# A fused convolution and gated feed-forward kernel: the conv bands built in 128x32 tiles, a late conv step, and the first weight slice loaded as fp32

## The chip, the cores and the metric

The kernel runs on one core of one Trainium2 chip. The metric is the device time of one execution in microseconds (us). Five engines matter: TensorE (PE in the profile, PEld for its weight loads), VectorE (DVE), ScalarE (ACT), GpSimd (POOL) and SyncE (SP, which here only issues DMAs). SyncE, ScalarE and GpSimd each issue their DMAs from the same in-order queue that holds their other instructions; for ScalarE the profile calls that queue ACTq.

## The reference

`x` is (8, 4096, 192), all in fp32. First comes a causal convolution over 7 taps with one set of softmax-normalised weights for each of 8 heads (24 channels each), then a gated feed-forward layer with 1536 hidden columns:

```python
w = exp(weight - max(weight)); w = w / (sum(w) + 1e-9)            # (8, 7)
out = einsum('hk,bskhg->bshg', w, windows(x_pad, 7))              # conv
x = out.reshape(B * S, D)
gate = maximum(x @ w_gate, 0); val = x @ w_val
return (gate * val) @ w_out                                       # (32768, 192)
```

## The kernel before

The 32768 tokens are worked in 16 units of 1024 tokens of each of two streams (batches 0 to 3 and 4 to 7). A unit runs `gate_val` for two windows of 512 tokens (matmuls of L621: for each of 12 blocks `f` of 128 hidden columns, gate and val, three chunks `c` of 64 channels, two streams `st`), then the projection (L643). The schedule is manual: each engine runs its instructions in the order in which the code is written, and the framework adds the semaphore waits.

The convolution of most windows is done by ScalarE, VectorE and GpSimd beside the matmuls of earlier units. For the first windows there is no earlier unit, so TensorE does it, with banded matrices. This head of the program is where the change lies. Its steps are:

- `load_raw` (L109) loads the first window's five overlapping pieces of x, called pieces 0 to 4 here, as fp32: 1, 0, 3, 4 by SyncE's queue and 2 by ScalarE's, after the small `w8`. In the tables of order the tiles `prod_86` to `prod_90` are pieces 0 to 4. `cast` (L119) turns each into fp16 on ScalarE, in the order 1, 0, 2, 3, 4.
- A small matmul (L203) spreads the conv weights, VectorE takes the maximum (L275), ScalarE the exponential `e` (L278) and its sum (L281), and VectorE makes `blocks` from them (L287 to L299), three pieces for heads 0-2, 3-5 and 6-7.
- L335: for each of the three `BANDS`, 8 matmuls with shifted selections from `Z` as weights (128x128) add `blocks` into a PSUM bank; VectorE copies each out to `bands` (L343).
- `conv_steps` (L391): 8 small matmuls (tiles of 32 columns) for each chunk `c` and piece; pieces 0, 1, 2, 3, 4 give columns 0, 106, 212, 318, 424 onwards of a 512-column window. Three chunks and five pieces make 120 matmuls.
- `evict` (L402) copies the three chunks from PSUM to `dense[0]`, chunk 0 and 2 on ScalarE and chunk 1 on VectorE.
- `load_w` (L224) loads the weights in four slices (columns 0-127, 128-383, 384-767, 768-1535) by GpSimd's queue, which turns fp32 into fp16, into partitions 0 to 63 of `Wg` and `Wv`. Stream 1 needs a copy in partitions 64 to 127: `both_halves` (L231) makes it, blocks 0 and 1 on VectorE, 2 to 9 on GpSimd (`pool_halves`), 10 and 11 by a DMA.
- `load_x` (L97) loads x for the second conv group (`xts[1]`, window 1 of unit 0) in two DMAs on GpSimd's queue, one for each stream. TensorE convolves it at block 10 of the first window (`CONV1`).

In the first block of the first window the L621 matmuls go by chunk: chunk 0 gate, chunk 0 val, chunk 1 gate, and so on, two matmuls (streams) at each step. So chunk 0's copy and both weight blocks are needed first, and chunk 1's copy two steps later.

Of the kernel before, what the change touches and what calls it, by code (L numbers as in the profile page):

```python
# [8 lines left out]
FP = mybir.dt.float32  # L9
# [6 lines left out]
def kernel(  # L16
# [12 lines left out]
    nc = tc.nc  # L29
# [7 lines left out]
    NCH = D // 64  # L37
    NBLK = D // 32
    NFF = DFF // 128
    WIN = 512  # L40
    NWIN = S // WIN
    SUB = 112
    STEP = 106
# [2 lines left out]
    GSUB = 5  # L46
    WARM = [(4, 4, 4, 1), (4, 4, 1)]
    STEPS0 = [1, 0, 2, 3, 4]
    CONV1 = 10


# [5 lines left out]
    LPOOL = NCH * WIN - LDVE  # L57
# [12 lines left out]
    apool = ctx.enter_context(tc.tile_pool(name="apool", bufs=1))  # L70
# [13 lines left out]
    def load_x(g, streams=range(2)):  # L84


        bp, toks = GROUPS[g]
        xt = staged(g // 3, g % 3).rearrange("p (j s d) -> p j s d", s=2, d=D)
        step = toks[1] - toks[0]
        rows = -(-(step + PAD) // 16) * 16  # L90
        for st in streams:
            src = bass.AP(
                tensor=x.tensor,
                offset=x.offset + ((bp + NB * st) * S + toks[0] - PAD) * D,
                ap=[[D, rows], [step * D, len(toks)], [1, D]],
            )
            nc.gpsimd.dma_start(out=xt[0:rows, 0 : len(toks), st, :], in_=src)  # L97
        return xt

    xts = {0: staged(0, 0).rearrange("p (j s d) -> p j s d", s=2, d=D)}  # L100
# [5 lines left out]
    def load_raw(queue, jj):  # L106
        lo = STEP * jj - PAD
        p0 = max(0, -lo)
        queue.dma_start(  # L109
            out=raw[jj][p0 : ROWS[jj], :].rearrange("p (s d) -> p s d", s=2),  # L110
            in_=bass.AP(
                tensor=x.tensor,
                offset=x.offset + (lo + p0) * D,
                ap=[[D, ROWS[jj] - p0], [NB * S * D, 2], [1, D]],
            ),
        )
# [7 lines left out]
    HR = 128 // H  # L124
# [5 lines left out]
    for jj in (1, 0, 3, 4):  # L130
        load_raw(nc.sync, jj)
    load_raw(nc.scalar, 2)

    zeros = const.tile([128, 128], F16)
    nc.vector.memset(zeros[:], 0.0)
# [21 lines left out]
    Z = const.tile([128, 256], F16)  # L157
# [3 lines left out]
    with nc.allow_low_precision("one of the terms is not zero"):  # L161
        nc.vector.tensor_reduce(
            out=Z[:, 112 : 112 + HR],
            in_=eye[:].rearrange("p (g i) -> p i g", i=HR),
# [4 lines left out]
        out=mask[:, :, 0],  # L169
        in_=eye[:].rearrange("p (g i) -> p g i", i=HR),  # L170
# [4 lines left out]
    Wg = const.tile([128, NCH, DFF], F16)  # L175
    Wv = const.tile([128, NCH, DFF], F16)
    Wo = const.tile([128, NFF, 3, 64], F16)
    nc.vector.memset(Wg[0:1, 0, 0:1], 0.0)

    held = psum.tile([128, 2, 512], FP, name="ps")  # L180

# [26 lines left out]
    for part, heads in zip(raised, BANDS):  # L208
        nc.tensor.matmul(  # L209
            out=part[:, 0 : SUB * len(heads)],  # L210
            lhsT=zeros[:],
            rhs=none(len(heads), SUB),
            start=True,
            stop=False,
# [6 lines left out]
    def load_w(s):  # L221
        cols = slice(CUTS[s], CUTS[s + 1])
        for src, dst in ((moe_w_gate, Wg), (moe_w_val, Wv)):
            nc.gpsimd.dma_start(  # L224
                out=dst[0:64, :, cols],
                in_=src.rearrange("(c p) f -> p c f", p=64)[:, :, cols],
            )

    def both_halves(copy, s, dst):
        cols = slice(HALVES[s], HALVES[s + 1])  # L230
        copy(out=dst[64:128, :, cols], in_=dst[0:64, :, cols])  # L231

    def pool_halves(s):
        both_halves(nc.gpsimd.tensor_copy, s, Wg)
        both_halves(nc.gpsimd.tensor_copy, s, Wv)
# [32 lines left out]
            )  # L268
        xes[b] = xe, head

    for s in range(2):
        load_w(s)

    mx = const.tile([128, 1], FP)
    nc.vector.tensor_reduce(  # L275
        out=mx[:], in_=spread[:, 0, 0:KW], axis=mybir.AxisListType.X, op=ALU.max, negate=True
# [34 lines left out]
    for s in range(2, 4):  # L311
        load_w(s)
    pool_halves(2)
    xts[1] = load_x(1, range(1))
    for s in (3, 4, 5):
        pool_halves(s)
    load_x(1, range(1, 2))
    for s in (6, 7):
        pool_halves(s)
# [8 lines left out]
    for part, heads, to, copy in zip(  # L328
        raised, BANDS, bands, [nc.vector.tensor_copy] * 3
    ):  # L330
        n = len(heads)
        for j in range(128 // HR):
            s0 = HR * j - PAD
            lo, hi = max(0, -s0), min(BW, SUB - s0)
            nc.tensor.matmul(  # L335
                out=part[:, 0 : SUB * n].rearrange("p (h t) -> p h t", t=SUB)[:, :, s0 + lo : s0 + hi],
                lhsT=Z[:, 112 - HR * j : 240 - HR * j],
                rhs=blocks[:, heads[0] : heads[0] + n, lo:hi],
                start=False,
                stop=(j == 128 // HR - 1),  # L340
                skip_group_check=True,
            )
        copy(out=to[:].rearrange("p h t -> p (h t)"), in_=part[:, 0 : SUB * n])  # L343
# [54 lines left out]
                            skip_group_check=True,  # L398
                        )

    def evict(copy, g, ps, c):
        copy(out=dense[0][:, g, c, :], in_=ps[:, 0, :])  # L402

    def conv(g):

# [301 lines left out]

    dense[0] = xcpool.tile([128, 2, NCH, WIN], F16, name="xc")
    first = [psum.tile([128, 2, 512], FP, name="ps") for _ in range(NCH)]
    for c, steps in ((0, STEPS0[:3]), (1, STEPS0[:2]), (0, STEPS0[3:]), (1, STEPS0[2:]), (2, STEPS0)):  # L710
        conv_steps(0, first[c], c, steps)
    both_halves(nc.vector.tensor_copy, 0, Wg)
    both_halves(nc.vector.tensor_copy, 0, Wv)
    for c, copy in enumerate((nc.scalar.copy, nc.vector.tensor_copy, nc.scalar.copy)):
        evict(copy, 0, first[c], c)
    both_halves(nc.vector.tensor_copy, 1, Wg)
    both_halves(nc.vector.tensor_copy, 1, Wv)
    xts[2] = load_x(2)
# [82 lines left out]
```

## Time and profile before

| | |
|---|---|
| median of 3 runs | 761.82 us (761.52 to 762.06) |
| span of the profiled execution (first to last instruction) | 760.2 us |
| the median over that span | 1.62 us more |
| PE busy | 756.0 us (99%), 13724 matmuls |
| DVE busy | 675.8 us (89%) |
| ACT busy | 610.1 us (80%) |
| POOL busy | 461.3 us (61%) |

The profile gives the span of the profiled execution and no time of its own beside it; the 1.62 us between the span and the median of the other runs lies before the first and behind the last instruction, or is the difference of two executions. A row of a timeline reads: start, length, engine, line, operation, output<-input with partitions x elements, how many instructions were merged, and in brackets the idle time of the engine just before it with what ended it. A line with x4 merges four instructions that follow each other.

### The profile page before, as it was taken

To read this page: it belongs to the slowest core of one execution; us is meant where nothing else is said; L and a number is where in the kernel's file an instruction comes from. 1 tells how busy PE (TensorE), PEld (TensorE's weight loads), DVE (VectorE), ACT (ScalarE), POOL (GpSimd) and SP (SyncE) were. 2 spreads that over 40 slices of the span, in tenths; PEclk is the share of its full clock that TensorE was granted. 3 is DMA by queue.
4 is the path that set the end of the run, shared out by engine and by line. 5 is a ranking of instruction groups with operands and counts; after the bars stand their busy time and mean duration, and the time that the engine had idled before them with its cause. 6 is when DMAs were issued, how large, how long until landed. Compare 5 with 4: busy or idle time off the path is not lost.

```text
span 760.2 us, 30531 instructions
## 1 busy us (share of the span) xinstructions
PE 756.0 (99%) x13724; PEld 454.8 (60%) x13724; DVE 675.8 (89%) x647; ACT 610.1 (80%) x680; POOL 461.3 (61%) x311
## 2 busy tenths in 40 slices
PE   9999999999999999999999999999999999999998
PEld 5555555565565666656666565666656556566658
DVE  7889989998998989989999899998999989897891
ACT  7897887878878788887877878788797887877671
POOL 8729649195591946829377392874919659193600
PEclk9999999999999999999999999999999999999999
DMA  8953532345324443333434324352243531240302
GB/s 142 137 69 92 79 85 46 43 96 75 85 44 52 97 66 85 55 61 83 60 85 71 66 67 55 85 85 69 56 49 93 77 86 44 23 100 9 85 2 85
DMA packets 153714, 54.07 MB, mean 71 GB/s; under 512 B 148912, under 2 KB 153584, under 8 KB 153584
## 3 DMA queue, kind: packets, MB, share of 16 engines
q1 hardware_dynamic: 117376, 37.78, 21.6%
q0 software_dynamic: 35808, 14.07, 16.4%
q8 instruction: 107, 1.75, 1.0%
q10 hardware_dynamic: 400, 0.27, 0.1%
q14 instruction: 23, 0.19, 0.1%
HBM read 28.98 MB, written 25.17 MB: 71 GB/s over the span
## 4 chain that ended last, share of the span: by engine, by line
PE 99%; DMA 0%; ACT 0%; issue 0%
PE ps L621 65%; PE ps L643 31%; PE ps L686 2%; PE ps L391 0%; DMA w<-in_weight_dram 0%; PE ps L193 0%; PE ps L335 0%; PE ps L414 0%; PE ps L209 0%; PE ps L203 0%; ACT out_s L697 0%; ACT L127 0%
## 5 line engine op out<-in xcount | busy, mean ns | idle before, releaser
L633 DVE TENSOR_TENSOR hT<-gr,ps 128x1024 f16<-128x1024 f16 (+1 forms) x385 | 469.1, 1219 | 35.5 <-ACT gr L632 8.7
L632 ACT ACTIVATE gr<-ps 128x1024 f16<-128x1024 f32 (+1 forms) x385 | 392.8, 1021 | 114.4 <-PE ps L621 114.4
L550 POOL TENSOR_TENSOR prod<-prod,prod 128x896 f32<-128x896 f32 x145 | 302.6, 2087 | 251.8 <-DVE prod L584 242.7
L621 PE MATMUL ps<-xc,Wg 64*64 64x512 f16 (+1 forms) x4464 | 318.4, 376 | 0.0
L621 PE MATMUL ps<-xc,Wv 64*64 64x512 f16 (+1 forms) x4464 | 318.3, 376 | 0.0
L643 PE MATMUL ps<-hT,Wo 64*64 64x512 f16 x4320 | 235.8, 376 | 0.0
L621 PEld LDWEIGHTS <-Wv 64*64 64x64 f16 (+1 forms) x4464 | 149.9, 106 | 98.5 <-DVE hT L633 0.3
L621 PEld LDWEIGHTS <-Wg 64*64 64x64 f16 (+1 forms) x4464 | 145.4, 107 | 103.4 <-issue 0.2
L643 PEld LDWEIGHTS <-Wo 64*64 64x64 f16 x4320 | 137.3, 107 | 95.7
L538 ACT ACTIVATE prod<-x_r,tap 128x1024 f32<-128x1024 f16 (+2 forms) x195 | 182.7, 1017 | 0.0
L574 DVE SCALAR_TENSOR_TENSOR acc<-x_r,tap,acc 128x1024 f32<-128x1024 f16 (+3 forms) x150 | 118.0, 854 | 0.0
L661 DVE STREAM_TRANSPOSE out_s<-ps 128x1024 f32<-128x1024 f32 x45 | 56.2, 1248 | 28.4 <-PE ps L643 24.4
L550 POOL TENSOR_TENSOR xc<-prod,prod 128x896 f16<-128x896 f32 x29 | 60.6, 2089 | 2.3
L479 POOL COPY x_p<-x_e 128x1536 f16<-128x1536 f16 (+1 forms) x32 | 42.2, 1351 | 0.0
L251 POOL DMA_DIRECT2D x_e<-in_x_dram x30 | 26.6, 890 | 0.0
L574 DVE SCALAR_TENSOR_TENSOR xc<-x_r,tap,acc 128x1024 f16<-128x1024 f16 (+3 forms) x30 | 25.2, 840 | 0.0
L563 ACT ACTIVATE acc<-x_r,tap 128x1024 f32<-128x1024 f16 (+3 forms) x30 | 22.5, 800 | 0.0
L656 ACT COPY turned_by<-ps 128x2 f32<-128x2 f32 x45 | 7.0, 155 | 16.8 <-PE ps L643 14.8
L686 PEld LDWEIGHTS <-hT 128*128 128x128 f16 x192 | 15.8, 98 | 0.4 <-issue 0.4
L686 PE MATMUL ps<-Wo,hT 128*128 128x192 f16 x192 | 16.0, 246 | 0.0
L697 ACT COPY out_s<-ps 128x768 f32<-128x768 f32 (+2 forms) x5 | 3.2, 638 | 12.7 <-PE ps L686 12.7
L697 DVE COPY out_s<-ps 128x192 f32<-128x192 f32 x1 | 0.4, 359 | 13.3 <-PE ps L686 13.3
(61 smaller groups left out, 74.4 us busy)
## 6 DMA issues: line engine op xcount, KB each, us to landing
out_dram<-out_s SPq DMA_DIRECT2D x125, 192.0 KB
x_e<-in_x_dram POOLq DMA_DIRECT2D x28, 384.0 KB, 6.3
x_r<-x_p SPq DMA_TRANSPOSE x116
prod<-in_moe_w_out_dram POOLq DMA_DIRECT2D x1, 576.0 KB, 8.7
prod<-in_x_dram SPq DMA_DIRECT2D x3, 168.0 KB
out_dram<-out_s SPq DMA_DIRECT2D x5, 96.0 KB
out_s<-in_x_dram POOLq DMA_DIRECT2D x2, 210.0 KB, 6.2
out_s<-in_x_dram POOLq DMA_DIRECT2D x2, 192.0 KB, 6.1
```

The source lines that it names most:

```text
L251: nc.gpsimd.dma_start(out=xe[:, 0:n, st, :, :].rearrange("p j c r -> p j (c r)"), in_=bass.AP(tensor=x.tensor, offset=x.offset + row * D, ...
L479: nc.gpsimd.tensor_copy(out=xp[:, js, :, st, :], in_=xe[:, js, st, :, :])
L538: nc.scalar.activation(out=both(prods[b, k], b, at, n), in_=shifted(b, c, k, t, n), func=ACTF.Copy, scale=tap[:, c, k : k + 1],)
L550: nc.gpsimd.tensor_tensor(out=acc if k < KW - 1 else xcs[b][:, w, :, :].rearrange("p c t -> p (c t)")[:, LDVE : NCH * WIN], in0=acc, in1=p ...
L563: nc.scalar.activation(out=both(accs[b], b, at, n), in_=shifted(b, c, 0, t, n), func=ACTF.Copy, scale=tap[:, c, 0:1],)
L574: nc.vector.scalar_tensor_tensor(out=result(b, at, n) if k == KW - 1 else both(acc, b, at, n), in0=shifted(b, c, k, t, n), scalar=tap[:, c ...
L621: nc.tensor.matmul(out=pss[i][q : q + M, st, :], lhsT=W[64 * st : 64 * st + 64, c, 128 * f + q : 128 * f + q + M], rhs=xcb[64 * st : 64 * ...
L632: nc.scalar.activation(out=gr[:, sts], in_=pss[0][:, sts], func=ACTF.Relu)
L633: nc.vector.tensor_tensor(out=h[:, f, sts], in0=gr[:, sts], in1=pss[1][:, sts], op=ALU.mult)
L643: nc.tensor.matmul(out=ps[64 * st : 64 * st + 64, b, :], lhsT=Wo[64 * r : 64 * r + 64, f, p, :], rhs=hs[b][64 * r : 64 * r + 64, f, st, :] ...
L661: nc.vector.transpose(out=o[:].rearrange("p t (b d) -> p b t d", b=2)[:, :, :, 32 * p : 32 * p + 32], in_=ps[:].rearrange("p b (t c) -> p ...
L686: nc.tensor.matmul(out=ps[:, i // 2, D * (i % 2) : D * (i % 2) + D], lhsT=h[:, f, st, 128 * q : 128 * (q + 1)], rhs=Wo[:, f, :, :].rearran ...
```

## The change

Four edits, all in the head:

1. The band matmuls (L335) use 32 columns of weights each, placed by `tile_position` in one quarter of the array, and write 32 partitions of the bank, in the order 0, 2, 4, 6, 1, 3, 5, 7 (`PLACED`), so that four neighbours lie in four quarters.
2. The first weight slice (128 columns) isn't loaded by GpSimd any more. SyncE issues two DMAs for gate and ScalarE two for val, fp32, one into each half of the partitions of a tile `sent` (it takes the buffer of `prod6`), and VectorE casts both halves at once into `Wg` and `Wv`, in place of its two `both_halves` copies. GpSimd's first weight DMA is now that of slice 1.
3. `conv_steps` for chunks 0 and 1 takes pieces 1, 0, 2, 3 first and piece 4 last. Chunks 0 and 1 are copied out in two parts: columns 0 to 317 and 318 to 511, on VectorE and ScalarE for chunk 0, on ScalarE and VectorE for chunk 1.
4. The first of the two `load_x` DMAs for the second group is issued behind blocks 3, 4, 5 of GpSimd's copies rather than ahead of them.

```diff
+    PLACED = [0, 2, 4, 6, 1, 3, 5, 7]
...
     load_raw(nc.scalar, 2)
+    sent = apool.tile([128, 2 * LPOOL], FP, name="prod6")[:, 0 : 2 * NCH * 128].rearrange(
+        "p (i c f) -> p i c f", i=2, c=NCH
+    )
+    for i, (queue, src) in enumerate(((nc.sync, moe_w_gate), (nc.scalar, moe_w_val))):
+        for half in (slice(0, 64), slice(64, 128)):
+            queue.dma_start(
+                out=sent[half, i],
+                in_=src.rearrange("(c p) f -> p c f", p=64)[:, :, 0:128],
+            )
...
-    for s in range(2):
-        load_w(s)
+    load_w(1)
...
     pool_halves(2)
-    xts[1] = load_x(1, range(1))
     for s in (3, 4, 5):
         pool_halves(s)
+    xts[1] = load_x(1, range(1))
     load_x(1, range(1, 2))
...
-        for j in range(128 // HR):
+        for j in PLACED:
+            q = HR * j // 32 * 32
...
-                lhsT=Z[:, 112 - HR * j : 240 - HR * j],
+                lhsT=Z[:, 112 - HR * j + q : 144 - HR * j + q],
                 rhs=blocks[:, heads[0] : heads[0] + n, lo:hi],
                 start=False,
-                stop=(j == 128 // HR - 1),
+                stop=(j % 2 == 1),
+                tile_position=(0, q),
...
-    for c, steps in ((0, STEPS0[:3]), (1, STEPS0[:2]), (0, STEPS0[3:]), (1, STEPS0[2:]), (2, STEPS0)):
+    for c, steps in ((0, STEPS0[:4]), (1, STEPS0[:4]), (0, STEPS0[4:]), (1, STEPS0[4:]), (2, STEPS0)):
         conv_steps(0, first[c], c, steps)
-    both_halves(nc.vector.tensor_copy, 0, Wg)
-    both_halves(nc.vector.tensor_copy, 0, Wv)
-    for c, copy in enumerate((nc.scalar.copy, nc.vector.tensor_copy, nc.scalar.copy)):
-        evict(copy, 0, first[c], c)
+    early_cols, late_cols = slice(0, 3 * STEP), slice(3 * STEP, WIN)
+    evict(nc.vector.tensor_copy, 0, first[0], 0, early_cols)
+    for i, dst in enumerate((Wg, Wv)):
+        nc.vector.tensor_copy(out=dst[:, :, 0:128], in_=sent[:, i])
+    evict(nc.scalar.copy, 0, first[0], 0, late_cols)
+    evict(nc.scalar.copy, 0, first[1], 1, early_cols)
+    evict(nc.vector.tensor_copy, 0, first[1], 1, late_cols)
+    evict(nc.scalar.copy, 0, first[2], 2)
```

What the built programs hold at the two places that matter is shown next; line numbers of the changed kernel are 1 to 13 higher. The names in brackets are the semaphores that an instruction waits for: `DMAHW0` to `DMAHW7` are eight counters that the DMAs of SyncE and ScalarE take in turn, `DMASW` those of GpSimd's DMAs, the others count an engine's finished instructions.

On ScalarE, at the program's start, stood before:

```order
L129 DMA w_93<-in_weight_dram 8x7
L109 DMA prod_88<-in_x_dram 112x2x192
L278 ACTIVATE e<-ps,mx 128x7 [waits DVE_49]
L281 ACTIVATE total,sm<-e 128x8 [waits Activation_49]
L119 CAST out_s<-prod_87 112x384 [waits DMAHW0_49]
L119 CAST out_s<-prod_86 118x384 [waits DMAHW1_49,Pool_49]
```

and stands now (`prod_100` is `sent`):

```order
L130 DMA w_93<-in_weight_dram 8x7
L110 DMA prod_88<-in_x_dram 112x2x192
L139 DMA prod_100<-in_moe_w_val_dram 64x3x128
L139 DMA prod_100<-in_moe_w_val_dram 64x3x128 [waits DMAHW1_49]
L287 ACTIVATE e<-ps,mx 128x7 [waits DVE_49]
L290 ACTIVATE total,sm<-e 128x8 [waits Activation_49]
L120 CAST out_s<-prod_87 112x384 [waits DMAHW0_49]
L120 CAST out_s<-prod_86 118x384 [waits Pool_49]
```

Two DMAs stand ahead of the exponential. There are now ten DMAs of SyncE and ScalarE for eight counters; the tenth is ScalarE's second, it shares the counter `DMAHW1` with the load of piece 0, and waits until that load has landed. The cast of piece 0 (`prod_86`) has lost its own wait for that load, since ScalarE has already waited.

On VectorE, behind the three copies of the bands, stood before:

```order
L343 CAST band_188<-ps 128x336 [waits PE_49]
L343 CAST band_189<-ps 128x336 [waits PE_49]
L343 CAST band_190<-ps 128x224 [waits PE_49]
L231 COPY Wg<-Wg 64x3x128 [waits DMASW0_49]
L231 COPY Wv<-Wv 64x3x128 [waits DMASW1_49]
L402 CAST xc<-ps 128x512 [waits PE_49]
```

and stands now:

```order
L356 CAST band_191<-ps 128x336 [waits PE_49]
L356 CAST band_192<-ps 128x336 [waits PE_49]
L356 CAST band_193<-ps 128x224 [waits PE_49]
L415 CAST xc<-ps 128x318 [waits PE_49]
L728 CAST Wg<-prod_100 128x3x128 [waits DMAHW6_49,DMAHW0_49]
L728 CAST Wv<-prod_100 128x3x128 [waits DMAHW7_49,DMAHW1_49]
L415 CAST xc<-ps 128x194 [waits Activation_49]
```

while ScalarE, behind its five casts, where two whole chunks stood, now holds:

```order
L120 CAST out_s<-prod_90 96x384 [waits DMAHW4_49]
L415 CAST xc<-ps 128x194 [waits DVE_49]
L415 CAST xc<-ps 128x318 [waits PE_49]
L415 CAST xc<-ps 128x512 [waits PE_49]
```

The second part of each chunk waits for the other engine's copy of its first part (`DVE_49` on ScalarE for chunk 0, `Activation_49` on VectorE for chunk 1), so the two parts of a chunk follow each other. The first part of chunk 0 waits for TensorE's count 107 in the built program: 35 up to the bands, 32 for chunk 0's four pieces, 32 for chunk 1's, and 8 for chunk 0's piece 4. So it waits for the whole chunk, piece 4 among it, and not for its own columns alone; the first part of chunk 1 likewise waits for 115.

More of the change, by code (lines that the diff above doesn't have):

```diff
@@ L177 @@
     Wo = const.tile([128, NFF, 3, 64], F16)
-    nc.vector.memset(Wg[0:1, 0, 0:1], 0.0)
+    nc.vector.memset(Wg[0:1, 0, 128:129], 0.0)
     held = psum.tile([128, 2, 512], FP, name="ps")
@@ L335 @@
             nc.tensor.matmul(
-                out=part[:, 0 : SUB * n].rearrange("p (h t) -> p h t", t=SUB)[:, :, s0 + lo : s0 + hi],
-                lhsT=Z[:, 112 - HR * j : 240 - HR * j],
+                out=part[q : q + 32, 0 : SUB * n].rearrange("p (h t) -> p h t", t=SUB)[
+                    :, :, s0 + lo : s0 + hi
+                ],
+                lhsT=Z[:, 112 - HR * j + q : 144 - HR * j + q],
                 rhs=blocks[:, heads[0] : heads[0] + n, lo:hi],
                 start=False,
-                stop=(j == 128 // HR - 1),
+                stop=(j % 2 == 1),
+                tile_position=(0, q),
                 skip_group_check=True,
@@ L399, in conv_steps, with evict @@
                         )
-    def evict(copy, g, ps, c):
-        copy(out=dense[0][:, g, c, :], in_=ps[:, 0, :])
+    def evict(copy, g, ps, c, cols=slice(0, WIN)):
+        copy(out=dense[0][:, g, c, cols], in_=ps[:, 0, cols])
     def conv(g):
```

## The prediction

> **What bounds the kernel now.** I read the chain that ended last first: it says which engine the end hangs on, and where that engine ever waited.
>
> ```profile
> PE 99%; DMA 0%; ACT 0%; issue 0%
> ...
> 7.81 13.22 PE ps L621 x120
> 21.03 1.64 PE ps L391 x120
> 22.66 18.28 PE ps L621 x168
> ...
> 88.61 15.54 PE ps L643 x288
> 104.15 31.09 PE ps L621 x575
> ...
> 710.22 31.08 PE ps L621 x576
> ```
>
> From 7.81 us on TensorE runs through without a wait that the chain shows, and each later unit has the same lengths, 31.08 and 15.54. So no edit of the head can gain or lose anything but by the moment at which the first L621 matmuls run, and whatever delays them goes to the end one for one. The two pieces ahead of the conv group (L391 at 21.03) bound what could be caught up. Next I read the timelines of ScalarE, VectorE and TensorE over the first 9 us, to see which wait ends last ahead of 7.81.
>
> ```profile
> 0.87 0.59 ACTq L129 DMA_DIRECT2D w<-in_weight_dram  x1
> 1.50 0.34 ACTq L109 DMA_DIRECT2D prod<-in_x_dram  x1
> 3.55 0.27 ACT L278 ACTIVATE e<-ps,mx 128x7 f32<-128x7 f32 x1 [1.25 <-DVE mx L275]
> 4.06 1.78 ACT L119 CAST out_s<-prod 112x384 f16<-112x384 f32 x4
> 6.18 0.51 ACT L119 CAST out_s<-prod 96x384 f16<-96x384 f32 x1 [0.34 <-DMA prod<-in_x_dram]
> 7.17 0.58 ACT L402 CAST xc<-ps 128x512 f16<-128x512 f32 x1 [0.48 <-PE ps L391]
> ...
> 5.56 1.22 DVE L343 CAST band<-ps 128x336 f16<-128x336 f32 x3 [0.26 <-PE ps L335]
> 6.81 0.39 DVE L231 COPY Wg<-Wg 64x384 f16<-64x384 f16 x1
> 7.44 0.69 DVE L402 CAST xc<-ps 128x512 f16<-128x512 f32 x1
> ...
> 4.97 1.22 PE L335 MATMUL ps<-blocks,Z 128*128 128x48 f16 x24
> 6.12 1.68 PE L391 MATMUL ps<-band,out_s 112*32 112x106 f16 x120
> 7.81 0.39 PE L621 MATMUL ps<-xc,Wg 64*128 64x512 f16 x2
> 8.24 0.40 PE L621 MATMUL ps<-xc,Wg 64*128 64x512 f16 x2
> ```
>
> The chain through the head: exponential at 3.55, band matmuls at 4.97, band copies from 5.56, conv from 6.12, chunk 0's copy on ScalarE from 7.17 to 7.75, first L621 matmul at 7.81, chunk 1's first at 8.24, 0.11 after VectorE's copy of chunk 1 ends at 8.13. The weights came in time and were copied by VectorE ahead of that. The exponential started when the maximum came, and ScalarE had been idle 1.25 us for it.
>
> **The wait on ScalarE.** The order shows a DMA ahead of the exponential that waits for the load of piece 0. When that load lands is in the view of line L119 over 4.1 to 4.3 us, because the cast of piece 0 had the same wait, and as the only cast with two waits it kept one as a row of its own in ScalarE's queue.
>
> ```profile
> L119 ACTq EVENT_SEMAPHORE  x1: 17/17/17, 4.1 to 4.1; - x1
> ...
> L109 SPq DMA_DIRECT2D prod<-in_x_dram x4: 398/454/458, 0.8 to 2.3; - x4
> L109 ACTq DMA_DIRECT2D prod<-in_x_dram x1: 339/339/339, 1.5 to 1.5; - x1
> ```
>
> The wait ended at 4.1; before, it held nothing, since the first cast ran until about then. Now the DMA behind it takes 0.34 to 0.59 us to issue (the rows of loads from DRAM, 0.59 that of `w`); I take 0.40, near most of them. So the exponential starts at about 4.55, **1.0 us later**. Behind it wait its sum, all five casts, and through VectorE the whole making of the bands.
>
> **The bands and the conv.** All else equal the band matmuls start at 4.97 + 1.0 = 5.97. The 24 took (1.22 - 0.2 for the length of the last) = 1.02 us start to start, 0.043 each, so the 8 of one band 0.34. Now four run side by side; L391's tiles of the same width ran at (1.68 - 0.21)/120 = 0.012 each, so two rounds of four are about 0.1. The first band copy then starts 0.59 - 0.25 = 0.34 behind the matmuls, at 6.31. It can't gain more: the copies follow each other every 0.42 (1.22 for three, the last 0.38), so they start at 6.31, 6.73, 7.15 and end at 6.81, 7.23, 7.53. **Gain of this edit: 0.25 us.**
>
> Conv starts 0.06 behind the first copy, at 6.87. Chunk 0's four pieces (32 matmuls at 0.0125) end at 7.27, chunk 1's start at 7.29 with the second band and end at 7.69, chunk 0's piece 4 at 7.79. The casts don't hold it: five of them, 0.42 apart, from 4.06 + 1.0 on, the last ends at 7.26. Nor does the load of piece 4, which landed at 6.18 before (two weight DMAs now compete with it).
>
> **The copies out.** Their lengths come from copies of near sizes:
>
> ```profile
> L343 DVE CAST band<-ps 128x336 f16<-128x336 f32 x2 | 0.9, 502 | 0.3 <-PE ps L335 0.3
> ...
> 755.30 0.48 ACT L697 COPY out_s<-ps 128x384 f32<-128x384 f32 x1 [1.18 <-PE ps L686]
> 756.29 0.36 DVE L697 COPY out_s<-ps 128x192 f32<-128x192 f32 x1 [13.32 <-PE ps L686]
> 757.28 0.32 ACT L697 COPY out_s<-ps 128x192 f32<-128x192 f32 x1 [1.50 <-PE ps L686]
> ```
>
> As the order stands, the parts form one string, all behind piece 4: 0.25 from TensorE's last matmul to the copy (as from the eighth band matmul, 5.31, to the copy at 5.56), VectorE's first part of chunk 0 8.04 to 8.52 (0.48), ScalarE's second 8.57 to 8.89 (0.32), ScalarE's first of chunk 1 to 9.26 (0.42, overlapping by 0.05), VectorE's second from 9.31 to 9.67 (0.36), and 0.06 later, at 9.73, chunk 1's first L621 matmul, which stood at 8.24. That is **1.49 later**. Before, chunks 0 and 1 were copied whole and side by side; the split alone lengthens the way from chunk 0's end to that matmul to 1.94 us.
>
> VectorE's two casts of the weights lie between its copies. The trace has no fp32 cast from SBUF to SBUF on VectorE; the nearest are the fp16 copy (0.39, half the partitions, same columns) and the fp32 cast from PSUM (0.50). At 0.45 each they run from 8.5 to 9.4 and end just as chunk 1's string needs VectorE: no cost; at 0.50 0.1 more. Nothing is gained where two copies went, since these had been hidden behind the conv.
>
> **The weight loads.** Gate must have landed by 8.5, val by 9.0.
>
> ```profile
> Wg<-in_moe_w_gate_dram POOLq DMA_DIRECT2D x1, 48.0 KB, 3.7
> Wv<-in_moe_w_val_dram POOLq DMA_DIRECT2D x1, 48.0 KB, 3.2
> Wv<-in_moe_w_val_dram POOLq DMA_DIRECT2D x1, 144.0 KB, 4.9
> out_s<-in_x_dram POOLq DMA_DIRECT2D x2, 210.0 KB, 6.2
> ...
> 33.54 0.51 POOL L501 TENSOR_TENSOR front_acc<-x_r,tap 128x192 f32<-128x192 f16 x1
> ```
>
> SyncE has issued gate by about 2.72 + 2 x 0.45 = 3.6, ScalarE the last of val by 4.55; with 3.2 to 4.9 us to land val comes between 7.4 (from the start of its issue) and 9.4. I take it as hidden by the string above; at the late end it costs 0.4. SyncE's tap DMAs go behind two more issues; the first reader of `tap` (L501) runs at 33.5, so some us of delay cost nothing.
>
> **x requested later, and GpSimd.** TensorE met GpSimd's copies closely once: blocks 2, 3 and 4 stood 1.34 and 1.32 apart, where 31.08 us for the 24 blocks of a unit make 1.295.
>
> ```profile
> 10.42 0.83 PE L621 MATMUL ps<-xc,Wg 64*128 64x512 f16 x6
> 11.76 0.81 PE L621 MATMUL ps<-xc,Wg 64*128 64x512 f16 x6
> 13.08 0.83 PE L621 MATMUL ps<-xc,Wg 64*128 64x512 f16 x6
> ...
> 13.74 0.79 POOL L97 DMA_DIRECT2D out_s<-in_x_dram  x1
> ...
> 20.96 1.71 PE L391 MATMUL ps<-band,out_s 112*32 112x106 f16 x120
> ```
>
> With TensorE 1.4 us later those waits go, 0.07 us. x for the second group was last requested at 13.74 and took 6.2 us (the 210 KB row above); two requests of 0.8 us each from about 14 on have landed by 21.8 at that rate, and conv now asks at 22.4. No cost; without the delay elsewhere, at 20.96, it would be up to 0.8.
>
> **Sum.** +1.0 (the wait) + 0.74 (copies out as one string, piece 4 ahead of chunk 1's and 2's end) - 0.25 (bands) - 0.07 (waits that vanish) = **+1.4 us**, on the span 760.2 to 761.6, and on the median 761.82, which lies 1.62 above that span, 763.2. That is 0.18% slower. A measurement of this kernel can tell about 0.2%, or 1.5 us, from no change, so the sign is surer than the verdict.
>
> **Rivals.** *TensorE stays slow.* A matmul of 512 columns takes longer in the head than later:
>
> ```profile
> L193 PE MATMUL ps<-const-bfloat16-1.0 128*128 128x512 bf16 x5 | 2.5, 618 | 0.8 <-PEq L785 0.8
> L335 PE MATMUL ps<-blocks,Z 128*128 128x66 f16 x12 | 0.9, 243 | 0.0
> L621 PE MATMUL ps<-xc,Wg 64*128 64x512 f16 x6 | 1.2, 379 | 0.0
> ```
>
> The faster pace was there by 6.12 (conv's 0.012), not yet at 4.97 (0.043 for a band matmul), though the granted clock is printed as full throughout. In the new order TensorE idles about 5.0 to 5.97 and 6.1 to 6.87, which it didn't. If the pace rises only later, conv runs at half: 32 + 32 + 8 matmuls at 0.025 end at 8.67 in place of 7.79, +0.9, so 764.1; each us of L621 at half pace adds 0.5, so 3 us of it would make 765.6. For it: the rise came behind some 5 us of nearly unbroken filler (L193) and band matmuls; against: TensorE still works as before up to about 5, two thirds of the 3 us ahead of 6.1. Chance 0.25. The Trainium skill, page "TensorE: Matmul & The Clock Gate", section "Part 1: The HAM clock gate (the "warmup" mystery)", names this a clock gate that opens after one busy window of about 3.4 us, free-running; by that rule, read strictly, the window around 6 us no longer counts and the time is 764.1 or more, while the sum above has it open as before.
>
> *The weights come late* (0.12): val at 9.4 puts its cast's end at 9.9 and the second L621 step at 9.96, where the forecast has it by about 9.5: +0.4, 763.6.
>
> *The wait costs nothing, and the change is not slower by an amount that can be told* (0.10). It decides if piece 0 lands by about 3.1, a full us earlier, or if ScalarE's queue lets the exponential pass. Then the exponential is at 3.55, piece 4's cast ends at 6.69 and chunk 0 at 6.85; with 1.94 chunk 1's matmul is at 8.79, +0.55 - 0.07: 762.3. Against: the same load landed at 4.1 with less traffic, and queues are in order.
>
> *Faster* (0.04): only if the parts also overlap; at best some 0.3, 761.5, since L621 started 0.11 behind its last copy.
>
> **Chances and range.** The forecast has 0.49. Its own spread is 762.6 to 763.8 (landing of piece 0 and issue 0.2 each way, copies 0.2, run to run 0.3). Of it a third lies above 763.34, the bound of 0.2%, of the slow pace nearly all, of late weights most: 0.17 + 0.24 + 0.09 = 0.50 slower, 0.46 within, 0.04 faster. The range 762.2 to 765.0 takes in the free wait and the slow pace through conv and leaves the rest out.
>
> **What would show it.** Right: a wait on ScalarE's queue until about 4.1 and `e` near 4.5; band copies from 6.3; chunk 1's second copy on VectorE ending near 9.7, and the second gate matmuls of L621 just behind; equal lengths of all later stages. Wrong: `e` at 3.55 (the wait is free); conv's 120 matmuls at 0.025 each (pace); VectorE idle ahead of its weight casts for a DMA; or TensorE waiting for GpSimd's copies or for x at block 10.

## The result, and the profile after

The changed kernel takes 764.93 us (764.55 to 765.80, 5 runs) against 761.82 (761.52 to 762.30, 5 runs): +3.1 us, a ratio of 1.0033 with a 95% interval of 1.0021 to 1.0044 (the ratio on record is not the quotient of the two medians, which is 1.0041). That is slower by more than the 0.2% that a measurement can tell, inside the range, and 1.7 us above the predicted 763.2. The span of the profiled execution is 763.5 (before 760.2).

The timelines of ScalarE, VectorE and TensorE over the first 13 us of the changed kernel (start, length, engine, line, operation; in brackets the idle time ahead and what ended it) answer to those shown of before:

```profile
1.89 0.72 ACTq L139 DMA_DIRECT2D prod<-in_moe_w_val_dram  x1
4.14 0.60 ACTq L139 DMA_DIRECT2D prod<-in_moe_w_val_dram  x1
4.79 0.27 ACT L287 ACTIVATE e<-ps,mx 128x7 f32<-128x7 f32 x1 [2.49 <-DMA prod<-in_x_dram]
9.44 1.14 ACT L415 CAST xc<-ps 128x194 f16<-128x194 f32 x3 [1.82 <-DVE xc L415]
...
6.56 1.22 DVE L356 CAST band<-ps 128x336 f16<-128x336 f32 x3
8.92 0.49 DVE L415 CAST xc<-ps 128x318 f16<-128x318 f32 x1 [1.14 <-PE ps L404]
9.33 0.54 DVE L728 CAST Wg<-prod 128x384 f16<-128x384 f32 x1
9.79 0.55 DVE L728 CAST Wv<-prod 128x384 f16<-128x384 f32 x1
...
3.11 0.56 PE L213 MATMUL ps<-w,rows 8*128 8x7 f32 x2 [0.71 <-DMA w<-in_weight_dram]
6.21 0.65 PE L345 MATMUL ps<-blocks,Z 128*32 128x48 f16 x24 [0.72 <-DVE blocks L308]
7.12 2.75 PE L404 MATMUL ps<-band,out_s 112*32 112x106 f16 x120 [0.27 <-DVE band L356]
9.93 0.61 PE L634 MATMUL ps<-xc,Wg 64*128 64x512 f16 x2
12.07 0.44 PE L634 MATMUL ps<-xc,Wv 64*128 64x512 f16 x2
12.34 0.81 PE L634 MATMUL ps<-xc,Wg 64*128 64x512 f16 x6
```

The first matmul of the feed-forward layer (L621, now L634) moved from 7.81 to 9.93, by 2.12. Three differences make it: the exponential comes 1.24 later (3.55 to 4.79), the way from it to conv is 0.24 shorter (2.57 to 2.33), and that from conv's start to the first L634 is 1.12 longer (1.69 to 2.81). The chain of waits goes through VectorE there. From conv's start to the first copy of chunk 0 it is 1.80 (to 8.92) where it was 1.05 (to 7.17): conv's 120 matmuls took 2.75 us instead of 1.68, and 72 of them stand ahead of that copy now, 56 before. From the copy to the first L634 it is 1.01 instead of 0.64, since VectorE casts gate's weights behind its copy (9.33 to 9.87) and the matmul waits for that. Then the first block, six steps of two matmuls, takes 2.41 us (9.93 to 12.34) instead of 1.32 (7.81 to 9.13): +1.09. That is 3.21 by the second block. The chain of waits shows it nearly unchanged behind that:

```profile
9.33 0.55 DVE Wg L728
...
9.93 14.30 PE ps L634 x120
24.22 1.52 PE ps L404 x120
25.74 18.24 PE ps L634 x168
...
713.24 31.08 PE ps L634 x576
```

25.74 stood at 22.66 (+3.08), 713.24 at 710.22 (+3.02), and the lengths are those of before. So the loss arises ahead of the second block.

### The profile page after: what moved, and what is told of

It is laid out like the page before. It is cut to its first block, busy times and chain, and to the rows that moved or that the text cites. A ratio compares the mean times of both kernels' runs of the same rounds, so it can differ in the third digit from the quotient of the medians.

```text
span 763.5 us, 30537 instructions
## 1 busy us (share of the span) xinstructions
PE 757.7 (99%) x13724; PEld 426.2 (56%) x13724; DVE 676.7 (89%) x648; ACT 610.4 (80%) x681; POOL 459.6 (60%) x309
## 3 DMA queue, kind: packets, MB, share of 16 engines
HBM read 29.17 MB, written 25.17 MB: 71 GB/s over the span
## 4 chain that ended last, share of the span: by engine, by line
PE 99%; DMA 0%; DVE 0%; issue 0%; ACTq 0%; ACT 0%; SPq 0%; DVEq 0%
PE ps L634 65%; PE ps L656 31%; PE ps L699 2%; PE ps L404 0%; DMA prod<-in_x_dram 0%; PE ps L427 0%; DVE blocks L308 0%; ACTq L139 0%; DVE Wg L728 0%; DVE band L356 0%; SPq L110 0%; DVE prod L296 0%; ACT out_s L710 0%; DVE blk L303 0%; ACT e L287 0%
## 5 line engine op out<-in xcount | busy, mean ns | idle before, releaser
L634 PE MATMUL ps<-xc,Wg 64*64 64x512 f16 (+1 forms) x4464 | 315.0, 376 | 0.1
L634 PE MATMUL ps<-xc,Wv 64*64 64x512 f16 (+1 forms) x4464 | 314.8, 376 | 0.0
L634 PEld LDWEIGHTS <-Wv 64*64 64x64 f16 (+1 forms) x4464 | 143.6, 106 | 105.5 <-issue 0.4
L634 PEld LDWEIGHTS <-Wg 64*64 64x64 f16 (+1 forms) x4464 | 133.8, 107 | 115.3 <-issue 0.6
L656 PEld LDWEIGHTS <-Wo 64*64 64x64 f16 x4320 | 126.3, 107 | 106.7
```

What stands on the lines that cost most here:

```text
L634: nc.tensor.matmul(out=pss[i][q : q + M, st, :], lhsT=W[64 * st : 64 * st + 64, c, 128 * f + q : 128 * f + q + M], rhs=xcb[64 * st : 64 * ...
L656: nc.tensor.matmul(out=ps[64 * st : 64 * st + 64, b, :], lhsT=Wo[64 * r : 64 * r + 64, f, p, :], rhs=hs[b][64 * r : 64 * r + 64, f, st, :] ...
```

## The experiments

Every kernel was compared with the kernel before on its own chip, where that one had medians of 762.42 to 762.56. "Above" is the difference of the medians; the ratio has its 95% interval. No trace of the kernel before was kept from these comparisons: where a trace of an experiment is set against before, it is the first profile, of a kernel that took 761.82 then, some 0.6 to 0.7 us less than beside the experiments. Differences between traces can therefore be larger than those of the table.

| kernel | median, us | above | ratio |
|---|---|---|---|
| the change again | 764.64 | +2.1 | 1.0029 (1.0019 to 1.0039) |
| second edit (weights) alone | 766.33 | +3.8 | 1.0045 (1.0033 to 1.0058) |
| the change without the second edit | 763.06 | +0.5 | 1.0002 (0.9993 to 1.0011) |
| first edit (bands) alone | 762.80 | +0.2 | 1.0000 (0.9992 to 1.0009) |
| the change without the third edit (copies) | 764.52 | +2.0 | 1.0027 (1.0016 to 1.0037) |
| the change without the fourth edit (x) | 766.13 | +3.7 | 1.0050 (1.0037 to 1.0063) |
| no wait, all weights by SyncE | 765.86 | +3.4 | 1.0040 (1.0026 to 1.0055) |
| no wait, one load moved | 764.03 | +1.6 | 1.0028 (1.0017 to 1.0040) |
| TensorE's gaps filled | 764.15 | +1.7 | 1.0022 (1.0013 to 1.0031) |
| all by SyncE, gaps filled | 764.21 | +1.7 | 1.0027 (1.0018 to 1.0035) |
| one load moved, gaps filled | 764.09 | +1.7 | 1.0026 (1.0015 to 1.0037) |
| the kernel before, less filler | 763.30 | +0.9 | 1.0013 (1.0004 to 1.0022) |

The intervals of the rows near 1.0025 overlap, so what parts them is read from their traces.

### Which edit it is

**The change again**, with no edit.

> The changed kernel itself, run beside its single parts on their chip. 2.7 to 3.5 us above the kernel before, with the exponential at 4.8 to 5.2 and, if TensorE's faster pace comes late because of the idle gaps, conv's 120 matmuls in 2.7 us again. If conv takes 1.7 us here, the pace hangs on chance in each execution, not on the gaps, and the time of such executions is 1.5 to 2 us lower.

It is 2.1 us above, less than the first time, with an interval that covers most of the first one; by the ratios the two agree (1.0033 and 1.0029). The profiled execution has conv at 2.75 us again, but the first block reached the faster pace after three matmuls (10.54 0.38 for a step, where the first profile had 0.63 until 11.64). So the slow stretch ends at different moments.

**The second edit alone**, on the kernel before:

```diff
+    for i, (queue, src) in enumerate(((nc.sync, moe_w_gate), (nc.scalar, moe_w_val))):
...
-    for s in range(2):
-        load_w(s)
+    load_w(1)
...
-    both_halves(nc.vector.tensor_copy, 0, Wg)
-    both_halves(nc.vector.tensor_copy, 0, Wv)
+    for i, dst in enumerate((Wg, Wv)):
+        nc.vector.tensor_copy(out=dst[:, :, 0:128], in_=sent[:, i])
```

> The second edit alone: the fp32 loads of the first weight slice and the casts in place of GpSimd's loads, all else as before. Theory (this edit holds ScalarE, makes TensorE idle and so slow): exponential at 4.8 to 5.1, wide band matmuls at 6.2 to 6.5, conv at half pace; the copies are whole and side by side, but VectorE's two casts (0.54 us each) stand ahead of chunk 1's copy and the weights land at 8.5 to 9.0, so chunk 1's copy ends at 10.3 to 10.7; 2.0 to 3.0 us above before. Rival (the loss comes from the split copies and the late piece 4, the wait on ScalarE being covered): within 0.7 us of before.

+3.8, more than the whole change and more than the 2.0 to 3.0 expected. The exponential is at 5.28, conv takes 2.54; and a loss that no theory had stands in VectorE's and TensorE's timelines:

```profile
9.08 0.55 DVE L721 CAST Wg<-prod 128x384 f16<-128x384 f32 x1 [0.59 <-DMA prod<-in_moe_w_gate_dram]
...
10.72 2.80 DVE L240 COPY Wg<-Wg 64x384 f16<-64x384 f16 x1
...
13.58 0.82 PE L629 MATMUL ps<-xc,Wg 64*128 64x512 f16 x5 [1.59 <-DVE Wg L240]
```

The copy of block 1's weights lasted 2.80 us, and TensorE stood 1.59 us for it. The run without the fourth edit, below, takes this up.

**The change without the second edit:** the loads and copies of before, with edits 1, 3 and 4.

```diff
-    load_w(1)
+    for s in range(2):
+        load_w(s)
...
-    for i, dst in enumerate((Wg, Wv)):
-        nc.vector.tensor_copy(out=dst[:, :, 0:128], in_=sent[:, i])
+    both_halves(nc.vector.tensor_copy, 0, Wg)
+    both_halves(nc.vector.tensor_copy, 0, Wv)
```

> The change without its second edit: GpSimd loads the first weight slice again, VectorE copies its halves; bands in narrow tiles, late piece 4 and split copies, late request of x stay. Theory: no wait on ScalarE, exponential near 3.55, band copies from 5.2, conv from 5.8, in 1.7 to 2.2 us; what is left is the string of half copies, worth 0.4 to 1.0, less 0.25 for the bands: 0.1 to 0.8 us above before. Rival (the split copies and piece 4 make most of the loss): 1.5 us or more above before. Rival (the bands' idle gaps alone keep TensorE slow): conv at 2.7 us and 1.5 to 2.5 above before.

+0.5, a ratio not to be told from 1. The exponential is at 3.66 with nothing ahead of it. So the loss hangs on the second edit; the other three together cost 0.8 us at most by the interval. But in the profiled execution (763.09, near the median) conv ran at the slow pace that the second rival named, though not at its price, and with no DMA ahead of the exponential:

```profile
6.08 2.75 PE L396 MATMUL ps<-band,out_s 112*32 112x106 f16 x120 [0.37 <-DVE band L348]
...
9.59 0.40 PE L626 MATMUL ps<-xc,Wg 64*128 64x512 f16 x2
```

The two steps ahead of 9.59 took 0.61 each. So the slow pace does not need the wait on ScalarE. TensorE idled here 0.47 us for w and 0.37 us between the narrow bands and conv; which of the three remaining edits makes conv slow was not taken apart, and what the slow pace costs in this version is within the 0.8 us.

**The first edit alone.**

> The first edit alone: the band matmuls in four tiles of 32 columns. Theory: they take 0.5 to 0.65 us instead of 1.22, the band copies start 0.25 earlier, conv at 5.8 to 5.9, and the time falls by 0.1 to 0.3 us, within what can be told. Rival (TensorE works less ahead of conv, so its faster pace comes later): conv or its first part at 0.023 us for a matmul, 0.3 to 2 us above before.

No difference. The bands did come sooner: in its timeline the first band copy starts 1.71 us behind the exponential (3.15 to 4.86), where 2.01 stood before. What comes next takes it back:

```profile
5.66 0.92 ACT L120 CAST out_s<-prod 112x384 f16<-112x384 f32 x2 [0.64 <-DMA prod<-in_x_dram]
...
5.42 2.20 PE L396 MATMUL ps<-band,out_s 112*32 112x106 f16 x120 [0.24 <-DVE band L348]
```

Conv began earlier and lasted longer, since the cast of piece 3 had to wait for its load. Part of this is chance: w had landed earlier in this execution (its matmul ran at 2.34, in the profile of before at 2.76), so the exponential was 0.40 earlier, while piece 3 came later (its cast ran at 5.66; before, the first four casts ran on without a wait until 5.84). One profile doesn't tell how often the loads bind.

**The change without the third edit:** whole copies, pieces in the order of before, the weight casts ahead of them.

> The change without its third edit: pieces of x in the order of before, chunks 0, 1 and 2 copied out whole, on ScalarE, VectorE and ScalarE. The wait stays, so the exponential stays near 4.8. Theory: the string of half copies is worth 0.4 to 0.7 us: chunk 1's first matmuls come about 0.6 earlier than at 10.79, the time is 764.2 to 764.5. Rival (the split copies cost nothing, since in the slow pace the first block of the feed-forward layer is bound by its own matmuls, 0.43 us for each step of two): 764.8 to 765.1. A second rival (late piece 4 is what the split hides): slower than the change, 765.2 or more.

+2.0 where the change has +2.1: the split is worth nothing that shows. In the split order VectorE's two casts lie between its two copies; in this one they stand ahead of chunk 1's copy (9.06 and 9.53, the copy at 9.99), behind a wait for gate's load until 9.06. Both ways chunk 1 is there at about 10.6. TensorE was at the slow pace in this run too (steps of 0.61, 0.64 and 0.59 us up to 11.33) and came to chunk 1 later than its copy, so the run doesn't tell what the string of copies costs at the faster pace; the run with the gaps filled, below, does.

**The change without the fourth edit:**

```diff
-    for s in (3, 4, 5):
-        pool_halves(s)
     xts[1] = load_x(1, range(1))
+    for s in (3, 4, 5):
+        pool_halves(s)
```

> The change without its fourth edit: x for the second group requested ahead of GpSimd's copies of blocks 3, 4, 5, as before. In the run of the second edit alone VectorE's copy of block 1 began while GpSimd issued this request and took 2.80 us instead of 0.3 to 0.6, until GpSimd's train of copies had a gap, and TensorE waited 1.6 us for it. Theory (VectorE's and GpSimd's copies shut each other out, and the later request is what lets them take turns): the copy of block 1 takes 2 us or more, TensorE waits in block 1, 4.2 to 4.9 us above before. Rival (the place of the request costs nothing, as the prediction had it): 2.6 to 3.3 us above before.

+3.7, less than the 4.2 to 4.9 expected, with its five runs between 765.81 and 766.38: slower than the change by 1.6 us (by the run of the change here) or 0.6 (by the first), with intervals that overlap a little. Timelines of VectorE, TensorE and GpSimd:

```profile
10.71 2.48 DVE L241 COPY Wg<-Wg 64x384 f16<-64x384 f16 x1
...
13.24 0.82 PE L634 MATMUL ps<-xc,Wg 64*128 64x512 f16 x5 [1.05 <-DVE Wg L241]
...
9.89 0.86 POOL L98 DMA_DIRECT2D out_s<-in_x_dram  x1
10.75 0.52 POOL L241 COPY Wg<-Wg 64x384 f16<-64x384 f16 x1
11.19 0.52 POOL L241 COPY Wv<-Wv 64x384 f16<-64x384 f16 x1
...
12.99 0.50 POOL L241 COPY Wv<-Wv 64x384 f16<-64x384 f16 x1
```

VectorE's copy starts at the end of GpSimd's request and lasts nearly as long as the six GpSimd copies behind it. In the change, with no request between GpSimd's copies, VectorE's took 0.54 and 0.52 among them:

```profile
10.63 0.54 DVE L241 COPY Wg<-Wg 64x384 f16<-64x384 f16 x1
```

So the later request, an edit that the prediction priced at nothing, spares the change about 1 us, by TensorE's wait of 1.05. That the two engines shut each other out of the memory is an inference from the overlap; no run took GpSimd's copies away, and why VectorE gets in among them in one order and not in the other stays open. Nor are GpSimd's copies alone enough to explain it: in the run of the second edit alone VectorE's copy began at 10.72, during GpSimd's request (10.30 to 11.16) and 0.43 us ahead of GpSimd's next copy, longer than the 0.28 us that it takes undisturbed. A request by itself doesn't always hold it either: in the kernel before the same copy took 0.28 us from 8.16 while GpSimd requested weights (7.77 to 8.40). The Trainium skill, page "SBUF — State Buffer", section "SBUF: two separate sides", has GpSimd and some VectorE instructions (those in a two-port mode or with two SBUF inputs) share one pair of ports under an exclusive lock, with the loser blocked for the whole instruction. These rows agree that one engine holds up the other, but not in the length: a GpSimd copy takes 0.50 us, and VectorE's was held for 2.48. That VectorE's copy is of that kind no run here shows.

### Inside the second edit: the wait, the pace, the landing

**The wait, first attempt:** all four loads on SyncE.

```diff
-    for i, (queue, src) in enumerate(((nc.sync, moe_w_gate), (nc.scalar, moe_w_val))):
+    for i, (queue, src) in enumerate(((nc.sync, moe_w_gate), (nc.sync, moe_w_val))):
```

> Undoes the wait alone: all four loads of the first weight slice stand on SyncE's queue, so ScalarE's queue holds no DMA ahead of the exponential that waits for piece 0. Theory (wait plus copies' string plus TensorE's slow pace): the exponential, at 4.79 in the changed kernel and 3.55 before, is back at 3.6 to 3.9 (3.9 if the small load w still lands at 2.97, as in the changed kernel, rather than at 2.62). The band copies start near 5.6, conv near 6.2. If conv still runs at 0.023 us for a matmul, the first matmul of the feed-forward layer is at 8.9 and the time is 764.0; if TensorE's faster pace is back with the shorter idle gaps, it is at 8.0 to 8.3 and the time 762.3 to 762.8. Rival (the fp32 weights and their casts hold VectorE): the first matmul stays at 9.5 or later with a DMA as what VectorE waits for, and the time stays at 764.5 or more.

The rival's time came out: the exponential is at 3.15, and nothing is gained. Its runs lie between 763.80 and 767.20, and the profile is of one of the slowest, 767.13; in it val lands last. Its timelines of VectorE and TensorE:

```profile
8.93 0.55 DVE L728 CAST Wg<-prod 128x384 f16<-128x384 f32 x1 [0.69 <-DMA prod<-in_moe_w_gate_dram]
10.64 0.55 DVE L728 CAST Wv<-prod 128x384 f16<-128x384 f32 x1 [1.16 <-DMA prod<-in_moe_w_val_dram]
...
9.54 0.61 PE L634 MATMUL ps<-xc,Wg 64*128 64x512 f16 x2 [1.30 <-DVE Wg L728]
11.26 0.61 PE L634 MATMUL ps<-xc,Wv 64*128 64x512 f16 x2 [1.11 <-DVE Wv L728]
```

The view of the same run by stretches (stretch, length, busy times of PE, PEld, DVE, ACT and POOL with their instructions, granted clock, DMA share, GB/s):

```profile
6.00:8.00 2.00, 1.15 (x96) 0.99 (x96) 0.48 (x2) 0.51 (x1) 1.41 (x4) 1.00 1.18 195
8.00:10.00 2.00, 0.69 (x26) 0.19 (x10) 0.80 (x2) 1.14 (x3) 0.82 (x2) 0.62 1.21 201
10.00:12.00 2.00, 0.89 (x6) 0.38 (x6) 1.30 (x4) 0.00 (x0) 0.50 (x1) 0.50 1.18 205
```

It also tells what the slow pace most likely is. The granted clock falls to 0.50 behind a stretch in which TensorE worked 1.15 of 2 us, and there a step of two matmuls takes 0.61, the same 0.61 that the change shows where its clock is printed as 1.00. The wait for val is not in every execution: in the run with the same loads and the gaps filled, below, val's cast ran at 8.89 without one.

**The wait, second attempt:** only val's upper half moves to SyncE.

```diff
+            queue = nc.scalar if i == 1 and half.start == 0 else nc.sync
```

> The change with one of its four loads moved: ScalarE issues only val's lower half, SyncE gate's two halves and val's upper half, so ScalarE's queue no longer waits for piece 0, and the waits that remain stand on SyncE. Everything else, the bytes among it, is as in the change. Theory 1 (the loss has several limits at nearly one height: the wait, TensorE's slow pace, and the landing of the fp32 weights): exponential at 3.5 to 3.9 instead of 4.7, but gate and val land at 8.5 to 9.5 as before, VectorE waits for them, the first matmul of the feed-forward layer comes at 9.0 to 9.6, and the time is still 1.7 to 2.5 us above before. Theory 2 (the wait is the cause, the weights are hidden as the prediction had it): first matmul at 8.0 to 8.8, 0.6 to 1.2 us above before.

Theory 1. The exponential is back at 3.68, 1.1 us earlier than in the change, and the time falls by half a us by the medians (+1.6 against +2.1), by the ratios (1.0028 and 1.0029) by nothing that can be told:

```profile
3.68 0.27 ACT L288 ACTIVATE e<-ps,mx 128x7 f32<-128x7 f32 x1 [1.37 <-DVE mx L285]
6.75 0.51 ACT L120 CAST out_s<-prod 96x384 f16<-96x384 f32 x1 [0.73 <-DMA prod<-in_x_dram]
...
8.76 0.55 DVE L729 CAST Wg<-prod 128x384 f16<-128x384 f32 x1 [0.37 <-DMA prod<-in_moe_w_gate_dram]
9.27 0.55 DVE L729 CAST Wv<-prod 128x384 f16<-128x384 f32 x1
...
9.37 0.39 PE L635 MATMUL ps<-xc,Wg 64*128 64x512 f16 x2 [0.90 <-DVE Wg L729]
```

VectorE waits for gate, and TensorE idles 0.90 us for its cast.

**The pace:** the change with matmuls that serve nothing in TensorE's three gaps.

```diff
-    WARM = [(4, 4, 4, 1), (4, 4, 1)]
+    WARM = [(4, 4, 4, 1, 4, 2), (4, 4, 1)]
...
+    hold(4, 4)
...
+    hold(2, to=spread[:, 1])
```

> Keeps the change as it is, wait included, and adds matmuls without a use in TensorE's three idle gaps of the head (2.40 to 3.11, 5.33 to 6.21 and 6.86 to 7.12 us). Theory: the faster pace comes before conv, its 120 matmuls take 1.7 us instead of 2.75, the first block of the feed-forward layer 1.3 to 1.8 instead of 2.4, and the time falls by 1.5 to 2.0 us to 762.9 to 763.4, though the exponential stays near 4.8. Rival (the pace has nothing to do with the gaps, but with the new forms of the matmuls, 32 columns wide, or with the transfers running beside them): conv stays at 2.7 us and the time at 764.5 to 765.3.

Conv took 1.57 and the first block 1.59 us (9.68 to 11.27), as expected; the forms and the transfers are the same, so the pace follows TensorE's own use. The time did not follow as expected: it came out 1.7 above before, against the change's +2.1 (+3.1 the first time), where a fall by 1.5 to 2.0 was expected. Piece 0 landed only at 4.53 in this execution (exponential at 5.18), and VectorE's string of copies and casts is what bounds next:

```profile
7.62 1.57 PE L408 MATMUL ps<-band,out_s 112*32 112x106 f16 x120
9.68 0.39 PE L638 MATMUL ps<-xc,Wg 64*128 64x512 f16 x2 [0.49 <-DVE Wg L732]
10.14 0.39 PE L638 MATMUL ps<-xc,Wv 64*128 64x512 f16 x2
10.40 0.39 PE L638 MATMUL ps<-xc,Wg 64*128 64x512 f16 x2
...
10.00 0.35 DVE L419 CAST xc<-ps 128x194 f16<-128x194 f32 x1
```

The first step waits for gate's cast. The second comes 0.46 behind the first, 0.06 after val's cast (9.54 to 10.08), and the third, chunk 1's, 0.05 after VectorE's second copy ends at 10.35; later steps stand 0.22 apart. In the change TensorE came to chunk 1 only at 10.79, 0.20 after the same copy had ended (10.24 and 0.35 long): the slow pace had hidden the string.

**The pace on the kernel before:** three matmuls without a use taken out.

```diff
-    WARM = [(4, 4, 4, 1), (4, 4, 1)]
+    WARM = [(4, 4, 4, 1), ()]
```

> The kernel before with one thing taken away: the three matmuls without a use that TensorE runs behind the spreading of w (1.1 us of work). No wait, copy or load changes. Theory (TensorE's pace rises only behind a stretch of nearly unbroken work): it idles about 1 us more ahead of the bands, conv and perhaps the first block of the feed-forward layer run at half pace in most executions, 0.5 to 2.0 us above before. Rival (the pace rises by the clock alone, however TensorE is used): within 0.3 us of before, conv at 1.7 us.

+0.9 (11 runs, 762.76 to 764.08). In the profiled one conv takes 2.75 us and the first steps of the feed-forward layer 0.61 and 0.64, as in the change, though no wait, copy or load was touched:

```profile
6.42 2.75 PE L391 MATMUL ps<-band,out_s 112*32 112x106 f16 x120
9.11 0.61 PE L621 MATMUL ps<-xc,Wg 64*128 64x512 f16 x2
```

From conv's start TensorE works on without a gap in this run, in both profiles of the change and in that of the change without the second edit, and the first faster step comes 3.5 to 5.0 us behind it (6.42 to 10.77, 7.12 to 12.07, 6.97 to 10.54, 6.08 to 9.59). The page "TensorE: Matmul & The Clock Gate" of the Trainium skill, section "Part 1: The HAM clock gate (the "warmup" mystery)", has a free-running window of about 3.4 us that must be busy before the clock rises. These four lengths agree with it, none being shorter, and a window whose place differs from execution to execution would also fit their spread; no run here shows the window itself.

**Wait and pace together**, once with all loads on SyncE:

> Both: the four weight loads on SyncE's queue, and matmuls without a use in the first gap (while w is awaited) and between the bands and conv; the gap ahead of the bands should have closed by itself. Theory: exponential at 3.6 to 3.9, conv from 6.2 in 1.7 us, first matmul of the feed-forward layer at 8.1 to 8.5, the rest of the loss being the copies' string: 762.1 to 762.7. If the wait and the pace add up as in the theory, it takes back 2.2 to 2.8 of the 3.1 us. Rival (weights late): val, now issued last, lands at 8.5 or later and VectorE waits for it ahead of its second cast; 763.0 or more.

and once with the one load moved:

> As the kernel without the wait, with matmuls without a use in TensorE's gap ahead of w and between the bands and conv. Conv takes 1.6 to 2.2 us. Theory 1: VectorE then waits for the weights with nothing else late; first matmul of the feed-forward layer at 8.8 to 9.4, 1.2 to 1.9 us above before; that rest is the price of the fp32 loads. Theory 2: first matmul at 8.0 to 8.4, 0.2 to 0.6 above before.

Both are 1.7 above: no better than either repair alone, and not the 2.2 to 2.8 us back that the first was to bring. In the first, conv took 2.12 us and the first matmul came at 9.02, behind gate's cast (8.41 to 8.96). The second came out as its theory 1 had it, with the first matmul at 9.20. Conv runs at full pace there and has gaps; ScalarE and TensorE show why:

```profile
6.19 0.51 ACT L120 CAST out_s<-prod 112x384 f16<-112x384 f32 x1 [0.38 <-DMA prod<-in_x_dram]
7.26 0.51 ACT L120 CAST out_s<-prod 96x384 f16<-96x384 f32 x1 [0.56 <-DMA prod<-in_x_dram]
...
7.82 0.80 PE L407 MATMUL ps<-band,out_s 94*32 94x88 f16 x56 [0.42 <-ACT out_s L120]
9.20 0.39 PE L637 MATMUL ps<-xc,Wg 64*128 64x512 f16 x2 [0.58 <-DVE Wg L731]
```

Piece 4's cast starts at 7.26, for its load; before, it started at 6.18. Piece 4's load has more beside it now. The table of DMA issues of the changed kernel (queue, count, size of each):

```profile
prod<-in_moe_w_val_dram ACTq DMA_DIRECT2D x2, 96.0 KB
prod<-in_moe_w_gate_dram SPq DMA_DIRECT2D x2, 96.0 KB
```

That is 192 KB for each of gate and val, where one load of 48.0 KB stood. (The 48.0 KB are fp16 as written; what the page of the profile counts as read from HBM, the chip's DRAM, rose by 0.19 MB in all, from 28.98 to 29.17.) What remains of the loss with wait and pace gone is, as far as the traces tell, x and the weights landing later and VectorE's two casts, some 1.6 us together. The split of this rest is not shown. That the weights' bytes are what delays x was not isolated, by smaller loads for instance; GpSimd's loads of the next slice also start earlier now (2.84, before 4.27), and the filler keeps TensorE from the matmul that spreads w until 3.02, where it ran at 2.76 before.

## Why the prediction was partly right

- **The wait on ScalarE was right**, in its mechanism and nearly in size: it ended at 4.14, and the exponential came 1.24 later instead of 1.0, because the DMA took 0.60 to issue, not 0.40. Its price to the end was not 1.24: taken away, it gave back 0.5 by the medians against the change beside it and nothing by the ratios, because other limits stood close behind.
- **TensorE's slow pace was the mis-weighed step.** It stood among the rivals at 0.25, with 764.1 for conv and up to 765.6; 764.93 lies there. The sum kept the pace of before although the same sum held the idle gaps that undo it. In the first profile conv is 1.07 longer, of which about 0.6 (72 of 120 matmuls) delays the first copy, and the first block 1.09. Alone, in the kernel before with less filler, it costs +0.9; repaired in the change it gave back 0.4 to 1.4. The measured time lies inside the range because the range had taken in this rival; the sum itself fell short by 1.7.
- **The string of copies was right in its length and wrong as a term (+0.74) to be added.** From VectorE's first copy to the end of its second it took 1.67 (8.92 to 10.59), 1.63 in the sum. But TensorE at its slow pace came to chunk 1 0.20 behind the string's end, and with whole copies the change is as slow; with the gaps filled the string did bound chunk 1, as forecast. The +0.5 without the weights, near 0.74 - 0.25 = 0.49, is no confirmation: its interval holds zero, and its conv ran at the slow pace, which that sum leaves out.
- **The bands (-0.25) were right as a step**, 0.24 in the change and 0.30 alone, and gained nothing alone; in the one profile the loads of x bound conv next.
- **The weights were hidden, as forecast, by other delays only.** The casts started without a wait in the change (9.33). With the wait gone they became the bound at 8.76. Gate was to have landed by 8.5; in four runs its cast waited until 8.76 to 9.08, the earliest cast of all ran at 8.41. SyncE took 1.41 us for gate's two issues instead of 0.90, and the second landed 5.5 us after it began to be issued (3.56 to 9.06, second edit alone), longer than the 3.2 to 4.9 that the forecast took from GpSimd's loads. So in the forecast's own schedule they would often have been late.
- **The later request of x was priced at nothing, and spared about 1 us.** The forecast looked for who reads x, not for what GpSimd's copies do beside VectorE's. The waits that were to vanish (-0.07) hardly did: 3.21 at the second block are 3.19 at the second group's conv (21.03 and 24.22).
- **The sign was right**, and the stages behind the head kept their lengths.

No version was faster than the kernel before; the narrow bands alone and the change without the second edit can't be told from it. The cause is shown as far as the second edit; inside it, several limits lie within a us of each other, and no run took them all away.

## What to carry to other kernels

Where several chains end within a us of each other, a delay is not a term to be added, and removing it only shows the next; ask of each edit what the second and third latest chain would be. A wait that makes TensorE idle ahead of its first long stretch is paid for again in its pace, so reckon both as one case. When work goes to a DMA queue, count what the queue holds behind it and what bytes it puts beside the loads that are on the path.

## What was not expected of the hardware

The profile's granted clock reads 1.00 in the first microseconds whatever the pace; the length of a known matmul is what tells: a step of two took 0.61 us at a clock shown as 0.50 and 0.39 at full. And VectorE's copy of 64x384, 0.28 us in the run with one load moved, took 2.48 and 2.80 with a GpSimd request and a train of its copies beside it.
